# Forming only half of a real-input DFT's rows in the spectral layer, with the sums and differences on VectorE and GpSimd

## The chip, the cores and the metric

The kernel runs on one core of a Trainium2 chip. The metric is the time of one execution on the device in microseconds (us), as the median over several runs. The engines are named as the profile names them: PE is the TensorE matmul, DVE is VectorE, ACT is ScalarE, POOL is GpSimd. DMA is the memory transfer. SBUF holds the tiles that loads fill and operations read; PSUM holds what the matmuls write.

## The reference

The program runs four layers in the order A, B, A, B. Each adds its output to its input:

```python
x = x + A(layernorm(x), w_r, w_i)
x = x + B(layernorm(x), mem0, Wq, Wk, Wv, Wo)      # recurrent attention, not touched by the change
x = x + A(layernorm(x), w_r, w_i)
x = x + B(layernorm(x), mem0, Wq, Wk, Wv, Wo)

def A(x, w_r, w_i):                                 # x: 1 x 2048 x 640, bf16
    X = rfft2(x.astype(float32))                    # 2048 x 321 complex
    return irfft2(X * (w_r + 1j * w_i), s=(2048, 640)).astype(bfloat16)
```

## The kernel before

Layer A computes the transforms by matmuls with tables. The 2048 tokens are written as n = 16·s1 + s0. There are three stages, and the document uses these names throughout:

- **first transform**: normalise, then a transform over s1, with s1 on the partitions; the results lie in `YT`.
- **spectrum**: sixteen row groups `kg`; for each, the transform along d (640 to 321 frequencies), the transform across s0 (`K`), the complex filter, and the transform back across s0, to `UT`.
- **token stage**: for each of the sixteen s0, the transform back along d, the transform back over s1, the residual, the layernorm for layer B, and sums that layer B needs.

The first execution of layer A is called A1 here, the second A2. The parts that matter (cut; `...` marks the cuts):

```python
# first transform: 256 columns for each s0 (real and imaginary part of 128 rows)
nc.tensor.matmul(ps[...256 columns...], lhsT=xn[:, s0, ch * 128:(ch + 1) * 128], rhs=T[:, s0, :], start=True, stop=True)
...
# spectrum: 16 groups of 20 + 4 + 6 matmuls
for kg in range(16):
    ...
    for ch in range(5):
        for cin in range(2):
            lhsT = YT[:, ch, cin * 16 + kg, :, :].rearrange("p s k -> p (s k)")
            for cout in range(2):
                nc.tensor.matmul(ps[:, cout, 0:NF], lhsT=lhsT, rhs=Fd[:, ch, FD_IDX[(cin, cout)], :], start=(n == 0), stop=(n == 9))
            n += 1
    Z = ...; nc.scalar.copy(out=Z[:], in_=ps[:, :, 0:NF])
    ps3 = ...                                   # four matmuls with K: across s0
    nc.vector.tensor_tensor(out=t1[:], in0=ps3[:, :, 0:NF], in1=wr[:]..., op=ALU.mult)         # 642 elements
    nc.vector.tensor_tensor(out=t2[:], in0=ps3[:, ::-1, 0:NF], in1=wi[:]..., op=ALU.mult)      # 642 elements
    nc.vector.tensor_tensor(out=Xp[:, 0, 0:NF], in0=t1[:, 0, :], in1=t2[:, 0, :], op=ALU.subtract)
    nc.vector.tensor_tensor(out=Xp[:, 1, 0:NF], in0=t1[:, 1, :], in1=t2[:, 1, :], op=ALU.add)
    ...                                         # six matmuls back across s0
    nc.scalar.copy(out=UT[:, :, kg, :], in_=psuf[:, 0:768].rearrange("p (a k) -> p a k", k=8))
...
handoff.prefetch()                              # issues layer B's Wv, 5 x 1 MB, on GpSimd
# token stage: 12 + 8 matmuls for each s0; the residual is added on VectorE
for q in range(8):
    xr = wk.tile([128, 2, D], BF16, name="xr", tag="xr", bufs=4)
    nc.sync.dma_start(out=xr[:], in_=xs[:, 2 * q:2 * q + 2, :])
    xo = wk.tile([128, 2, D], BF16, name="xo", tag="xo")              # two buffers
    for t in range(2):
        ...
        nc.vector.tensor_tensor(out=xo[:, t, :]..., in0=psy[:, :, 0:320], in1=xr[:, t, :]..., op=ALU.add)
        _ln_stats(nc, st, mv, xo[:, t, :], t)
    nc.sync.dma_start(out=xd[:, 2 * q:2 * q + 2, :], in_=xo[:])       # the store of the layer's result
    ...
```

## Time and profile before

| | before |
|---|---|
| median of three runs (range) | 1765.64 us (1764.94 to 1770.21) |
| span of the profiled run | 1762.3 us |
| A1: first transform, spectrum, token stage | 40.4, 73.6, 58.7 us |
| A2: same (the first counted from the end of layer B) | 31.7, 73.5, 58.5 us |
| the rest, nearly all layer B | some 1400 us |

The head of the profile page gives the busy time of each engine and its share of the span:

```profile
span 1762.3 us, 36912 instructions
PE 1664.0 (94%) x14778; PEld 1136.0 (64%) x14779; DVE 863.2 (49%) x2432; ACT 816.8 (46%) x2234; POOL 222.9 (13%) x180
```

The share over the whole span says that PE is the limit, but what a change in layer A is worth is read from layer A's own stretches. In this view of stretches each line is one stretch: its bounds, its length, then the busy time of each engine (number of instructions), the granted PE clock, the share of time that the DMA engines were busy, and their GB/s.

```profile
core 0: us, PE busy (x) PEld busy (x) DVE busy (x) ACT busy (x) POOL busy (x), PEclk, DMA share, GB/s
0.00:40.40 40.40, 15.93 (x81) 9.75 (x83) 23.41 (x112) 21.41 (x30) 4.12 (x13) 0.82 0.68 157
40.40:114.00 73.60, 69.95 (x480) 44.62 (x479) 40.23 (x76) 22.67 (x32) 10.47 (x17) 0.98 0.61 152
114.00:172.70 58.70, 51.62 (x405) 33.46 (x405) 41.08 (x113) 25.90 (x48) 1.19 (x2) 0.97 0.56 206
914.00:987.50 73.50, 70.66 (x480) 44.85 (x480) 39.83 (x71) 21.98 (x32) 6.34 (x12) 0.96 0.44 94
```

In the spectrum (second line, and A2's in the fourth) PE is busy 70 of 73.6 us and DVE 40: PE is the limit, and removing matmuls there should pay. In the token stage PE is busy 51.6 of 58.7, and DVE 41. (A2's token stage, 58.5 us, reads the same.) The timeline shows the spectrum in detail; its columns are the start, the duration, the engine, the source line, the operation, output and inputs, and, in brackets, any idle time before it and what ended that.

```profile
74.94 0.30 PE L206 MATMUL ps<-Z,K 128*128 128x321 bf16 x1
75.22 2.36 PE L199 MATMUL ps<-Fd,YT 128*128 128x321 bf16 x16
...
79.25 0.30 PE L206 MATMUL ps<-Z,K 128*128 128x321 bf16 x1
```

One row group takes 79.25 − 74.94 = 4.31 us, and no line of it has a bracket: PE never waits. Sixteen of these make up the spectrum. On DVE, two lines of the same stretch:

```profile
75.43 0.83 DVE L210 TENSOR_TENSOR t<-ps,wr 128x642 f32<-128x642 f32 x1
76.17 0.82 DVE L211 TENSOR_TENSOR t<-ps,wi 128x642 f32<-128x642 f32 x1
```

Each lasts 0.82 to 0.83 us. Last, what the residual addition (L261) waited for, as time and number of times:

```profile
  DMA xr<-x: 9.2, 1
  DMA xr<-in_A_x_dram: 9.0, 1
```

In each layer A, DVE sits idle 9 us at the beginning of the token stage, until the first `xr` has landed. SyncE's queue (SPq) issued these loads 4.4 us after the first of the five `Wv` loads (108.8):

```profile
113.19 1.85 SPq L238 DMA_DIRECT2D xr<-in_A_x_dram  x4
```

PE itself lost only 1.99 us by it (1.55 in A2).

### The profile page before, as it was taken

The numbers are of one execution on the slowest core, as the hardware profiler recorded it, in microseconds if no ns is written. First come the engines' busy times: TensorE is split into PE (matmuls) and PEld (weight loads), VectorE is DVE, ScalarE is ACT, GpSimd is POOL, SyncE is SP. The second block draws the span as 40 slices with busy tenths as digits, with TensorE's granted clock in tenths as the row PEclk, the third lists the DMA queues.
The fourth block names the chain that finished last, engine by engine and source line by source line (L and its number), as shares of the span: only waits on it lengthen the run. The fifth ranks groups of instructions, "written<-read, shape, count | busy, mean of one in ns | idle before, by whom it ended". The sixth has DMA issues, their size and how long they took to land. (4 is left out here: it accounts for less than half of the span.)

```text
span 1762.3 us, 36912 instructions
## 1 busy us (share of the span) xinstructions
PE 1664.0 (94%) x14778; PEld 1136.0 (64%) x14779; DVE 863.2 (49%) x2432; ACT 816.8 (46%) x2234; POOL 222.9 (13%) x180
## 2 busy tenths in 40 slices
PE   4988899999999999999959889999999999999998
PEld 2655666666666666677736556666666666666776
DVE  5557255555455455443345572555555555555111
ACT  4334466656656656400023343656656656653000
POOL 0110011211211211200000000211211211211000
PEclk8999999999999999999979999999999999999999
DMA  6664034344344343374165540334434434424531
GB/s 144 158 239 157 14 105 148 115 148 148 116 147 148 117 149 123 113 236 146 53 158 99 202 142 17 129 121 137 151 124 137 152 122 136 145 108 140 186 128 32
DMA packets 148013, 233.11 MB, mean 132 GB/s; under 512 B 8480, under 2 KB 119664, under 8 KB 138096
## 3 DMA queue, kind: packets, MB, share of 16 engines
q1 hardware_dynamic: 141632, 203.72, 34.6%
q0 software_dynamic: 6192, 26.86, 6.0%
q8 instruction: 120, 1.97, 0.5%
q14 instruction: 69, 0.57, 0.1%
HBM read 191.30 MB, written 50.35 MB: 137 GB/s over the span
## 5 line engine op out<-in xcount | busy, mean ns | idle before, releaser
L755 DVE TENSOR_TENSOR P<-E,maskf 128x269 bf16<-128x269 bf16 (+5 forms) x576 | 199.6, 355 | 350.1 <-ACT E L754 350.1
L741 PE MATMUL psv<-wWv,hTf 128*128 128x256 bf16 x2720 | 340.4, 272 | 0.0
L678 PE MATMUL psk<-hTf,wWk 128*128 128x495 bf16 (+3 forms) x1600 | 324.3, 342 | 0.7 <-DVE hTf L970 0.7
L754 ACT ACTIVATE E<-pss 128x269 bf16<-128x269 f32 (+5 forms) x576 | 246.3, 429 | 152.0 <-PE pss L751 144.3
L678 PE MATMUL psq<-hTf,wWq 128*128 128x128 bf16 (+3 forms) x1560 | 314.3, 336 | 0.0
L743 ACT CAST V<-psv 128x512 bf16<-128x512 f32 (+1 forms) x288 | 162.0, 563 | 236.8 <-PE psv L741 236.8
L741 PEld LDWEIGHTS <-hTf 128*128 128x128 bf16 x2720 | 252.9, 98 | 24.6
L781 POOL TENSOR_TENSOR accS<-accS,sums_sb 128x634 f32<-128x634 f32 x64 | 98.3, 1536 | 931.3 <-ACT sums_sb L772 931.3
L734 DVE CAST KT<-psk 128x495 bf16<-128x495 f32 (+3 forms) x320 | 191.2, 598 | 41.9 <-PE psk L678 41.8
L502 PE MATMUL psx<-Wo_sb,oTxl 128*128 128x320 bf16 x1440 | 203.4, 299 | 0.0
L678 PEld LDWEIGHTS <-wWk 128*128 128x128 bf16 x1600 | 133.5, 97 | 96.6 <-issue 1.4
L751 PEld LDWEIGHTS <-KT 128*128 128x128 bf16 x1216 | 113.6, 98 | 116.4 <-issue 16.3
L678 PEld LDWEIGHTS <-wWq 128*128 128x128 bf16 x1580 | 127.0, 97 | 88.6 <-issue 1.1
L502 PEld LDWEIGHTS <-oTxl 128*128 128x128 bf16 x1440 | 140.9, 98 | 54.7
L719 ACT ACTIVATE QT<-psq 128x480 bf16<-128x480 f32 x300 | 170.0, 567 | 0.0
L751 PE MATMUL pss<-QT,KT 128*128 128x132 bf16 (+8 forms) x1216 | 159.5, 216 | 2.7 <-ACT E L754 2.6
L793 DVE TENSOR_TENSOR oT<-pso,oT 128x480 bf16<-128x480 f32 (+1 forms) x160 | 93.2, 583 | 60.3 <-PE pso L789 49.7
L789 PE MATMUL pso<-P,V 128*128 128x132 bf16 (+8 forms) x1216 | 120.1, 216 | 2.6 <-DVE oTmf L795 2.5
L516 DVE TENSOR_TENSOR xo<-psx,xr 128x320 bf16<-128x320 f32 x64 | 31.4, 490 | 177.1 <-PE psx L502 177.1
L793 DVE TENSOR_TENSOR oT<-pso,Rb 128x480 bf16<-128x480 f32 (+1 forms) x160 | 93.0, 581 | 48.9 <-PE pso L789 48.9
L199 PE MATMUL ps<-Fd,YT 128*128 128x321 bf16 x640 | 104.4, 306 | 4.4 <-DMA Fd<-cFd 2.8
L502 PE MATMUL psx<-Wo_sb,oT 128*128 128x320 bf16 x608 | 98.7, 302 | 4.1 <-DVE oT L793 4.1
(169 smaller groups left out, 1745.1 us busy)
## 6 DMA issues: line engine op xcount, KB each, us to landing
oT<-Rd SPq DMA_DIRECT2D x32, 1059.5 KB
Rb<-Rd SPq DMA_DIRECT2D x32, 1059.5 KB
oTx_d<-oT SPq DMA_DIRECT2D x60, 512.0 KB
oTxl<-oTx_d SPq DMA_DIRECT2D x18, 1024.0 KB
Wv_sb<-in_B_Wv_dram POOLq DMA_DIRECT2D x10, 1024.0 KB, 9.7
wWq<-in_B_Wq_dram SPq DMA_DIRECT2D x32, 320.0 KB
wWk<-in_B_Wk_dram SPq DMA_DIRECT2D x32, 320.0 KB
wWv<-in_B_Wv_dram SPq DMA_DIRECT2D x32, 320.0 KB
```

The costliest lines, as they stand in the source:

```text
L199: nc.tensor.matmul(ps[:, cout, 0:NF], lhsT=lhsT, rhs=Fd[:, ch, FD_IDX[(cin, cout)], :], start=(n == 0), stop=(n == 9))
L502: self.tc.nc.tensor.matmul(ps[:, 0:320], lhsT=lhs(h, k // 2 % 4), rhs=self.g["Wo_sb"][:, h, c0:c0 + 320], start=(h == 0), stop=(h == H - 1))
L678: nc.tensor.matmul(ps, lhsT=w[:, ch, hh * 128:(hh + 1) * 128], rhs=src[:, ch, lo:hi], start=(ch == 0), stop=(ch == 4))
L719: nc.scalar.mul(out=qv[:, :, 0:SEG], in_=x_view(ps, o, n)[:, :, 1:SW], mul=scale)
L734: nc.vector.tensor_copy(out=KTs[h % 2][:, lo:hi], in_=ps[:, 0:hi - lo])
L741: nc.tensor.matmul(ps[:, i * 256:(i + 1) * 256], lhsT=hT[:, ch, (t + i) * 128:(t + i + 1) * 128], rhs=w["Wv"][:, ch, :], start=(ch == 0), ...
L743: nc.scalar.copy(out=V[:, t:t + n, :].rearrange("p a b -> p (a b)"), in_=ps[:, 0:n * 256])
L751: nc.tensor.matmul(ps[:, off - o0:off - o0 + hi - lo], lhsT=KT[:, t * 128:(t + 1) * 128], rhs=QT[:, lo:hi], start=True, stop=True)
L754: nc.scalar.activation(out=E[:, 0:n], in_=ps[:, 0:n], func=ACTF.Exp)
L755: nc.vector.tensor_tensor(out=P[:, o0:o0 + n], in0=E[:, 0:n], in1=bs.mask[:, o0:o0 + n], op=ALU.mult)
L789: nc.tensor.matmul(pso[:, lo - q0:hi - q0], lhsT=V[:, t, (h % 2) * 128:(h % 2 + 1) * 128], rhs=P[:, off:off + hi - lo], start=(i == 0), st ...
L793: nc.vector.tensor_tensor(out=oT[:, s0 * SEG:(s0 + ns) * SEG].rearrange("p (s t) -> p s t", t=SEG), in0=po[:, :, 0:SEG], in1=pr[:, :, 0:SE ...
```

## The change

The input is real, so the transform over s1 and s0 has a symmetry: the rows for group 16 − j are conjugates of those for group j. The changed kernel forms only groups 0 to 8 of 16. The cosine and sine parts along d are computed once for each group, and their sums and differences give both the group and its mirror. The intent is to halve the matmuls along d and back along d. The price is elementwise work: a sum and a difference ahead of the transform across s0, and a sum and a difference after the filter. They go to VectorE and GpSimd. In the token stage the residual is added on PE, with an identity matrix, as the first two matmuls into the output's PSUM. In A1 the normalisation moves from VectorE to ScalarE, and the one-element copies that order a load after an earlier use of its buffer (the "gates", L108) do so everywhere. The core of the diff, with cuts:

```diff
 # first transform: 128 columns instead of 256
-        for j in range(4): nc.tensor.matmul(ps[... 256 columns], lhsT=xn[...], rhs=T[:, s0, :], ...)
+        for i in range(4): nc.tensor.matmul(ps[:, i, :], lhsT=xn[...], rhs=T[:, 4 * q + i, :], ...)
-                _ln_apply(nc, wk, mv, xt, xn[:, 4 * q:4 * q + 4, :], 4, eps_t, on_dve=True)
+                _ln_apply(nc, wk, mv, xt, xn[:, 4 * q:4 * q + 4, :], 4, eps_t)
...
 # spectrum: 8 steps j instead of 16 groups kg
+    def along_d(j, o):          # o=0 cosines, o=1 sines: 10 matmuls each; o=1 is copied to SBUF by ScalarE
+    def combine(j):
+        nc.vector.tensor_tensor(out=P[j][:, 0:2, :], in0=ac[:, :, 0:NF], in1=db, op=ALU.add)
+        nc.vector.tensor_tensor(out=P[j][:, 2:4, :], in0=ac[:, :, 0:NF], in1=db, op=ALU.subtract)
+    def across(j, sg):          # sg=0 the group, sg=1 its mirror: 4 matmuls each, into ONE buffer X
+    def filt(j, sg):            # two 642-element multiplications on VectorE for each sg
+    def products(j, sum_engine):
+        nc.vector.tensor_tensor(out=a[:, 0, :, :], in0=t1[j][:, :, 0, :], in1=t2[j][:, :, 0, :], op=ALU.subtract)
+        nc.gpsimd.tensor_tensor(out=a[:, 1, :, :], in0=t1[j][:, :, 1, :], in1=t2[j][:, :, 1, :], op=ALU.add)
+        if j:
+            sum_engine.tensor_tensor(out=sd[j][:, 0:2, :], in0=a[:, :, 0, :], in1=a[:, :, 1, :], op=ALU.add)
+            nc.gpsimd.tensor_tensor(out=sd[j][:, 2:4, :], in0=a[:, :, 0, :], in1=a[:, :, 1, :], op=ALU.subtract)
+    def back(j):                # for three chunks of frequencies: 4 matmuls into one of 2 buffers, 2 ScalarE copies
+        for j in range(8 + 3):
+            if j < 8:        along_d(j, 1)
+            if 1 <= j <= 8:  across(j - 1, 0); filt(j - 1, 0)
+            if j < 8:        along_d(j, 0); combine(j)
+            if 1 <= j <= 8:  across(j - 1, 1)
+            if j >= 3:       back(j - 3)        # and up to two late weight loads, issued on GpSimd
+            if 1 <= j <= 8:  filt(j - 1, 1); products(j - 1, nc.vector if j >= 7 else nc.gpsimd)
...
 # token stage: 6 + 6 matmuls for each s0
-    nc.vector.tensor_tensor(out=xo[:, t, :]..., in0=psy[:, :, 0:320], in1=xr[:, t, :]..., op=ALU.add)
+    for a in range(2):
+        nc.tensor.matmul(psy[:, a, 0:320], lhsT=g["ident"][:], rhs=xr[q][:, t, a * 320:(a + 1) * 320], start=True, stop=False)
+    ...                         # four matmuls with Ti
+    nc.scalar.copy(out=halves(xo[q][:, t, :]), in_=psy[:, :, 0:320])
```

The mirrored filter rows (`Wm`) are gathered by two indirect loads.

## The prediction

> **What bounds it now.** In the windows layer A takes 349 of 1762 us: A1 is 0-172.7 (first transform 40.4, spectrum 73.6, token stage 58.7), A2 884-1046 (15.0 waiting for xn, then 15.0, 73.5, 58.5). Layer B is untouched. In the spectrum PE is the limit: busy 69.95 of 73.6 us, DVE 40.2, ACT 22.7; the timeline repeats every 4.30 us, 16 times, with 30 matmuls, 0.137 us apart at 321 columns. In the token stage PE is busy 51.6 of 58.7, after a stall on the first residual load (DVE idle 9.0 us on DMA xr).
>
> **What changes.** Matmuls per layer: first transform 80 of 256 columns become 80 of 128; spectrum 16 x 30 become 8 x 40; tokens 16 x 20 become 16 x 12. PE work is then about 8 x (28 x 0.137 + 12 x 0.116) = 42 us in the spectrum and 16 x (1.64 + 0.34) = 32 us in the token stage.
>
> PE stops being the only limit of the spectrum. DVE gets seven 642-element operations per step j; two of that size take 826 and 815 ns now, so 5.8 us a step. (The Trainium skill, "VectorE: DVE Perf Modes", section on the SBUF-source errata: an fp32 add of two tensors takes (N+151)/0.96 ns, 826 for 642; the trace agrees.) GpSimd gets three adds; its 634-element add takes 1.536 us, so 4.65 us a step plus weight issues (0.5-0.9 each). The single X buffer makes a loop: filter half 0 (1.66), across half 1 (0.6), back with two PSUM buffers (1.9), along d (1.37), across half 0 (0.6), handovers: 6.3-6.5 us. Eight steps of 5.9-6.5 us, 4.5 to fill, about 10 to drain (last GpSimd difference, back(7), copy): 59 us against 73.6.
>
> Token stage: PE 2.15-2.3 us a row, ACT about 1.65 (two 0.69 copies), DVE 1.9, so PE still. The residual now goes first into PSUM, so PE itself waits for xr, issued only when the spectrum ends, beside 5 MB of Wv: 4-6 us lost, partly cold (the Trainium skill, "TensorE: Matmul & The Clock Gate", Part 1: half clock after an idle window of about 3.4 us[...]). Total 48 against 58.7.
>
> First stage: A1 moves the normalisation to ACT and splits the copies: about 33 against 40.4. A2 reads half the T table and its copies halve, but the mirrored filter is gathered ahead of Fd, and K is six times larger: the spectrum starts about 6 us earlier.
>
> **Sum.** A1 -33, A2 -31: 1765.6 - 64, about 1702 us (-3.6%). Nearly all is critical. Interval 1678 to 1728. Faster by over 2%: 0.93; within 2%: 0.06; slower: 0.01.
>
> **What would show it.** Spectrum windows of 55-63 us, DVE busy near 85%, PE 70-75% and waiting on DVE; GpSimd add near 1.55 us; token windows 45-50 us, PE about 75%, one wait on xr of 4-6 us; first spectrum matmul near 33 us in A1; later stages unchanged, shifted.
>
> **What would make it wrong.** GpSimd and DVE slowing each other (the products run together from SBUF), with GpSimd the limit at over 6.5 us a step; K or the gather landing late in A2; Wv or writes saturating DMA in the shorter token stage (13 MB in 48 us; 206 GB/s now); PE gaps dropping the clock to half through the spectrum. Upwards: steps of 5.8 us give another 5 us a layer.

## The result, and the profile after

The changed kernel took 1709.43 us (median of four runs, 1704.61 to 1711.07), the kernel before 1765.97 in the runs beside it. The ratio is 0.9671, with a 95% interval of 0.9645 to 0.9697: 3.3% faster. Ratios here and below are the mean time of one kernel's runs over the mean of the other's in the same rounds, so not quite the ratio of the medians quoted. The same file (e0 below) gave 1708.39.

The page and the stretches after, in the same views and columns:

```profile
span 1709.3 us, 35729 instructions
PE 1577.4 (92%) x14202; PEld 1085.8 (64%) x14203; DVE 838.0 (49%) x2315; ACT 809.5 (47%) x2327; POOL 288.9 (17%) x228
```

```profile
0.00:36.90 36.90, 11.47 (x81) 7.25 (x83) 23.64 (x86) 21.23 (x41) 6.61 (x19) 1.00 0.66 173
36.90:101.90 65.00, 48.85 (x320) 32.26 (x321) 43.83 (x58) 21.80 (x71) 38.28 (x31) 0.95 0.48 127
101.90:147.50 45.60, 32.97 (x277) 22.66 (x276) 27.93 (x97) 24.78 (x48) 3.74 (x7) 0.84 0.80 300
886.30:947.60 61.30, 48.66 (x320) 32.30 (x321) 46.41 (x57) 21.52 (x66) 34.53 (x26) 0.92 0.33 72
947.60:992.50 44.90, 32.47 (x277) 22.15 (x276) 27.54 (x97) 24.38 (x49) 3.86 (x7) 0.90 0.81 304
```

PE lost 86.6 us of busy time (1664.0 − 1577.4), and the span 53. The difference is in the stretches: in the spectrum PE is now busy 48.9 of 65 us and DVE 43.8 (67%; 76% in A2, where 85% was predicted), and no engine is full; in the token stage PE is busy 33 of 45.6. By stretch:

| us | A1 before | A1 after | predicted | A2 before | A2 after | predicted |
|---|---|---|---|---|---|---|
| first transform (A2: from layer B's end to the spectrum) | 40.4 | 36.9 | 33 | 31.7 | 26.1 | 25.7 |
| spectrum | 73.6 | 65.0 | 59 | 74.3 | 61.3 | 59 |
| token stage | 59.2 | 45.7 | 48 | 58.9 | 45.0 | 48 |
| transposes to layer B's first matmul | 13.6 | 13.2 | | 13.2 | 14.0 | |

(Here every bound is the start of the first matmul of its kind, so the A2 spectrum and the token stages are up to 0.8 us off the round bounds used above.) The differences add up to −26.1 and −31.7 us. Layer B's two passes add +4.0 and +0.8, though nothing in them was changed; together −53.0, the difference of the two profiled spans. Layer B's first pass varied from 693.9 to 703.4 us between the profiled runs that have the same instructions there. So stretches of layer A are compared below rather than totals alone, where a few us matter. Why layer B varies stays open.

The stretches vary too. In the profiles that have the same instructions there, the spectrum took 64.4 to 65.1 us in A1 and 61.2 to 62.0 in A2, A1's first transform 36.7 to 37.4, the transposes 13.2 to 14.1. Each edit below has one profile, so a difference under 1 us is not read as an effect.

**A step of the spectrum.** The step repeats every 6.13 us:

```profile
68.32 0.72 PE L326 MATMUL X<-YT,K 128*128 128x321 bf16 x4 [0.34 <-DVE t L334]
68.89 1.03 PE L360 MATMUL psu<-K,YT 128*128 128x256 bf16 x8
70.22 0.60 PE L360 MATMUL psu<-K,YT 128*65 128x256 bf16 x4 [0.30 <-ACT UT L362]
70.65 1.54 PE L301 MATMUL ab<-Fd,YT 128*128 128x321 bf16 x10
72.03 0.71 PE L326 MATMUL X<-YT,K 128*128 128x321 bf16 x4
72.58 1.53 PE L301 MATMUL ab<-Fd,YT 128*128 128x321 bf16 x10
74.45 0.72 PE L326 MATMUL X<-YT,K 128*128 128x321 bf16 x4 [0.34 <-DVE t L334]
```

PE waits twice in a step: 0.34 us at the second `across`, because `X` has one buffer and the filter (L334) must empty it, and 0.30 us at the last chunk of `back`, because that stage has two PSUM buffers and ScalarE must empty one. In the rest of the step, 5.48 us, PE is busy. DVE is not full either:

```profile
68.18 0.82 DVE L314 TENSOR_TENSOR YT<-ab,GT 128x642 bf16<-128x642 f32 x1
68.92 0.82 DVE L315 TENSOR_TENSOR YT<-ab,GT 128x642 bf16<-128x642 f32 x1
69.65 1.55 DVE L334 TENSOR_TENSOR t<-X,Wm 128x642 f32<-128x642 f32 x2
...
72.83 1.56 DVE L334 TENSOR_TENSOR t<-X,WX 128x642 f32<-128x642 f32 x2 [0.70 <-PE X L326]
```

Its operations last 0.82 us and start 0.735 us apart, so seven of them take 7 × 0.735 = 5.15 us, and DVE itself waits 0.70 us for the next `X`. The single `X` is a loop of PE and DVE waiting for each other in turn.

**The end of the spectrum.** From the first to the last matmul group that writes `X(j, 0)` (the first `across` of a step) the seven intervals take 40.5 us in A1 (43.03 to 83.50) and 41.1 in A2. After the start of the last one come 18.4 us in A1 and 14.5 in A2 before the token stage can begin; this holds the whole eighth step. In A1 most of this is one wait of PE:

```profile
92.14 1.26 PE L326 MATMUL X<-YT,K 128*128 128x321 bf16 x4 [7.92 <-DVE t L334]
```

PE waits for DVE's filter; DVE in turn waited for GpSimd, since the sum of step 6 (L345), which the kernel puts on DVE near the end, stands ahead of the next filter in DVE's queue and needs GpSimd's addition (L343):

```profile
89.78 0.83 DVE L345 TENSOR_TENSOR YT<-ac 128x642 bf16<-128x642 f32 x1 [5.14 <-POOL ac L343]
90.53 1.55 DVE L334 TENSOR_TENSOR t<-X,WX 128x642 f32<-128x642 f32 x2
```

And GpSimd had what that addition needs (the filter, done by about 83.5) nearly 5 us before it got there, because its queue is in order and was behind:

```profile
78.00 0.90 POOL L1181 DMA_DIRECT2D Wo_sb<-in_B_Wo_dram  x1 [2.71 <-ACT Wo_sb L108]
...
82.39 1.56 POOL L343 TENSOR_TENSOR GT<-t,t 128x642 f32<-128x642 f32 x1
84.47 0.58 POOL L1035 DMA_DIRECT2D maskf<-mask_f_B_f  x1 [0.52 <-ACT m L108]
...
87.62 0.57 POOL L1037 DMA_DIRECT2D m<-in_B_mem_dram  x1
88.20 1.55 POOL L343 TENSOR_TENSOR ac<-t,t 128x642 f32<-128x642 f32 x1
```

The line at 78.00 shows the start of it: the issue of a weight load waited 2.71 us for its gate, a ScalarE copy of one element (L108). So the arithmetic behind the load waited too. In A2 there are no `Wo` loads, and PE's wait is 4.00 instead of 7.92.

**GpSimd and VectorE slow each other.** Where a GpSimd operation and a VectorE operation with both inputs in SBUF start together, the one that starts second takes much longer. From A2, DVE then POOL:

```profile
926.51 2.21 DVE L342 TENSOR_TENSOR GT<-t,t 128x642 f32<-128x642 f32 x1
```

```profile
926.49 1.55 POOL L343 TENSOR_TENSOR GT<-t,t 128x642 f32<-128x642 f32 x1 [0.96 <-DVE t L334]
```

The subtraction that takes 0.83 us alone took 2.21. In the reverse order, at 95 us in A1, DVE's took 0.83 and GpSimd's addition 2.19 instead of 1.55. In both cases the pair needed 2.23 us from the first start to the last end, nearly the sum of both durations (0.83 + 1.55 = 2.38). DVE's filters, one of whose inputs is in PSUM, stayed at 0.81 to 0.83 us beside GpSimd work. The Trainium skill ("SBUF — State Buffer", section "SBUF: two separate sides") says that VectorE and GpSimd share a pair of SBUF ports, that a VectorE operation with two SBUF inputs needs it against a GpSimd operation that reads SBUF, and that it "is an exclusive lock, not a bandwidth split", the one that starts first holding it for its whole instruction. The trace agrees.

**The token stage.** The predicted wait of PE for `xr` was only 0.66 us. The first `xr` loads are now issued 0.5 us ahead of `Wv` (101.76) and not 4.4 us behind it:

```profile
101.27 5.58 SPq L256 DMA_DIRECT2D xr<-in_A_x_dram  x5
```

A larger wait came instead, and in ACT's timeline it stands like this:

```profile
120.48 0.69 ACT L241 CAST xo<-psy 128x640 bf16<-128x640 f32 x1 [8.58 <-DMA x<-xo]
```

ACT writes the fifth row of output, the first into a buffer `xo` that is used a second time, and waits 8.58 us until the store of its former content (`x<-xo`) has landed; PE, out of PSUM buffers behind it, idles 6.97 us (6.40 in A2). The groups view of L241 sums the waits up for the whole kernel:

```profile
  DMA x<-xo: 18.0, 3
```

The store was issued at 107.8; 5 MB of `Wv` had been issued from 101.8. From 104 to 120 us the DMA engines are fully busy, with 407 to 424 GB/s; in this stretch of 4 us PE does nothing at all:

```profile
116.00:120.00 4.00, 0.00 (x0) 0.00 (x0) 0.00 (x0) 0.00 (x0) 0.00 (x0) 0.52 1.07 418
```

In the kernel before, `Wv` was issued at 108.8 and the first store 16.1 us later, at 124.9, when most of `Wv` had landed; there it was the `xr` loads that stood behind `Wv`. After the change the store comes only 6.0 us after `Wv`. The Trainium skill ("DMA: Bandwidth & Descriptors", section "Issuing engines are not separate DMA queues") says that transfers issued by different engines run on the same 16 DMA engines and interleave; that agrees with a store issued by SyncE being slowed by loads that GpSimd issued. After the stall PE runs at half clock (0.26 to 0.27 us for a matmul, against 0.137), as the prediction expected after such a gap (6.97 us here). So long a gap is not always needed: in the kernel before, the matmuls at 116.6 also took 0.47 us instead of 0.30, after gaps of only 2.19 and 0.89 us.

### The profile page after: what moved, and what is told of

Same layout as the page of the kernel before. It is cut to its first block, busy times and chain, and to the rows that moved or that the text cites. A ratio compares the mean times of both kernels' runs of the same rounds, so it can differ in the third digit from the quotient of the medians. Undisturbed runs are those within 1.5% of the kernel's fastest.

```text
span 1709.3 us, 35729 instructions
## 1 busy us (share of the span) xinstructions
PE 1577.4 (92%) x14202; PEld 1085.8 (64%) x14203; DVE 838.0 (49%) x2315; ACT 809.5 (47%) x2327; POOL 288.9 (17%) x228
## 5 line engine op out<-in xcount | busy, mean ns | idle before, releaser
L902 PEld LDWEIGHTS <-V 128*128 128x128 bf16 x1216 | 92.4, 99 | 15.3 <-DVE oTmf L908 8.2
## 6 DMA issues: line engine op xcount, KB each, us to landing
Wv_sb<-in_B_Wv_dram POOLq DMA_DIRECT2D x10, 1024.0 KB, 13.2
```

The source lines that it names most:

```text
L902: nc.tensor.matmul(pso[:, lo - q0:hi - q0], lhsT=V[:, t, (h % 2) * 128:(h % 2 + 1) * 128], rhs=P[:, off:off + hi - lo], start=(i == 0), st ...
```

## The experiments

Twelve runs followed: eleven edits of the changed kernel, and the changed kernel once more (e0). Every one gave the right result. Diffs are against the changed kernel. "Stretches" are those of the table above. In short:

| kernel | median us (range) | ratio to before | 95% |
|---|---|---|---|
| changed | 1709.43 (1704.61–1711.07) | 0.9671 | 0.9645–0.9697 |
| e0, changed again | 1708.39 (1706.21–1710.08) | 0.9669 | 0.9655–0.9683 |
| e1, four `xo` | 1692.84 (1692.11–1694.89) | 0.9585 | 0.9572–0.9599 |
| e2, sums on GpSimd to the end | 1706.20 (1704.28–1708.83) | 0.9664 | 0.9649–0.9679 |
| e3, `Wo` issued by SyncE | 1711.09 (1707.47–1715.61) | 0.9691 | 0.9672–0.9710 |
| e4, residual on DVE | 1724.00 (1722.95–1726.36) | 0.9762 | 0.9748–0.9776 |
| e5, normalisation on DVE | 1704.52 (1703.16–1707.24) | 0.9653 | 0.9639–0.9668 |
| e6, `Wv` later | 1708.90 (1707.04–1713.03) | 0.9679 | 0.9663–0.9696 |
| e7, `back` split | 1711.17 (1707.27–1714.31) | 0.9688 | 0.9673–0.9704 |
| e8, nothing on GpSimd | 1721.37 (1719.51–1723.44) | 0.9749 | 0.9735–0.9763 |
| e9, e1+e2+e3+e7 | 1691.08 (1686.04–1693.67) | 0.9577 | 0.9563–0.9590 |
| e10, e1+e3+e7 | 1692.72 (1690.98–1696.41) | 0.9583 | 0.9569–0.9596 |
| e11, three `xo`, six `xr`, e2+e3+e5+e7 | 1706.93 (1702.38–1709.90) | 0.9658 | 0.9638–0.9678 |

### e1: four buffers for the output row pair

Theory: the token stage stalls on the second use of an `xo` buffer. Rival: DMA is simply full there, and another buffer only moves the wait.

```diff
-                xo[q] = wk.tile([128, 2, D], BF16, name="xo", tag="xo")
+                xo[q] = wk.tile([128, 2, D], BF16, name="xo", tag="xo", bufs=4)
```

> The token tile xo gets four buffers instead of two. Theory (ACT may not overwrite an xo buffer until its store has landed, and the store waits in the DMA queues behind 5 MB of Wv): the ACT wait on DMA x<-xo (8.6 us in A1 of the changed kernel, 18 us in all) nearly goes, the token windows of 45.6 and 44.9 us shrink to 38-40, the kernel is 10 to 14 us faster than the changed one (about 1697). Rival (DMA saturation itself paces the stage, whoever waits): the wait moves to the residual loads xr or to later stores, the token windows stay over 43 us and the time within 4 us of the changed kernel.

Measured: 1692.84 us, about 16.6 less than the changed kernel. The token stages fell from 45.7 and 45.0 to 38.3 and 38.1 us; the first transforms and the spectra stayed within 0.3 us. What L241 waited for, after the edit:

```profile
  DMA x<-xo: 1.7, 2
```

18.0 us became 1.7. What remains on PE is a wait of 2.08 and 1.98 us for `xr`. The two stretches explain 7.4 + 6.9 = 14.3 us of the total; the rest is inside layer B's variation. The theory holds as far as PE goes: with more buffers PE no longer waits for the store. That the store is slow because of the traffic is another matter, for e6.

### e2: the last sums on GpSimd as well

Theory: DVE's queue is blocked by the sum that waits for GpSimd.

```diff
-                products(j - 1, nc.vector if j >= 7 else nc.gpsimd)
+                products(j - 1, nc.gpsimd)
```

> The sums of the last two steps go back from VectorE to GpSimd. Theory (VectorE runs in order, and its sum of step 6 stands in front of the filter of step 7 and waits for GpSimd's add, which is late): DVE no longer idles 5.1 us on POOL, PE's wait of 7.9 us before the second half of step 7 falls under 3 us in A1, although GpSimd gets two adds of 1.3 us more; the spectrum windows (65.0 and 61.3 us) shorten by 1 to 4 us each. Rival (the move to VectorE did shorten the drain, as it was meant to): both windows grow by 1 to 3 us, because the last GpSimd difference comes later by one or two adds.

Measured: 1706.20 us. PE's wait fell from 7.92 to 1.95 us in A1 (4.00 to 3.07 in A2), but GpSimd then ends later, and PE waits 1.80 us for it. The spectrum is shorter by 1.2 and 2.0 us only. So the wait at L345 was really what made the 7.92, but removing it uncovers GpSimd's own backlog as the next limit. The total alone, 2 to 3 us lower with overlapping intervals, does not show it.

### e3: the Wo loads issued by SyncE

Theory: the weight loads in GpSimd's queue, with their gates, hold up the arithmetic.

```diff
-        nc.gpsimd.dma_start(out=g["Wo_sb"][:, 8 * q:8 * q + 8, :], ...)
+        nc.sync.dma_start(out=g["Wo_sb"][:, 8 * q:8 * q + 8, :], ...)
```

> The four Wo loads are issued from SyncE instead of GpSimd (they need no cast); only A1 has them. Theory (GpSimd's adds are late in A1 because its queue also issues these loads, each after a wait for a gate copied on ACT): the A1 spectrum window falls from 65.0 to about 61 us, that of A2 (61.3), with PE's longest wait near A2's 4.0 us; A2 unchanged; the kernel 3 to 5 us faster. Rival (the lock between VectorE and GpSimd[...] alone makes the stall): A1 stays at 64-66 us.

Measured: 1711.09 us in total, not resolved from the changed kernel. PE's wait in A1 fell from 7.92 to 4.97, the spectrum of A1 by 1.6 us (65.0 to 63.4); A2, which has no such loads, stayed at 61.2. I had expected about 4 us. The trace says why: the `Wo` issues are gone, but the next load, of the mask, now holds the queue:

```profile
85.74 0.57 POOL L1035 DMA_DIRECT2D maskf<-mask_f_B_f  x1 [2.31 <-ACT m L108]
```

So the theory is half right: issues in that queue do cost, but removing one kind of them uncovers the next.

### e4: the residual back on VectorE

This undoes one part of the change. Theory: PE has time for two more matmuls a row, DVE does not have it for a 0.82 us addition.

```diff
-            for a in range(2):
-                nc.tensor.matmul(psy[:, a, 0:320], lhsT=g["ident"][:], rhs=xr[q][...], start=True, stop=False)
-            nc.scalar.copy(out=halves(xo[q][:, t, :]), in_=psy[:, :, 0:320])
+            nc.vector.tensor_tensor(out=halves(xo[q][:, t, :]), in0=psy[:, :, 0:320], in1=halves(xr[q][:, t, :]), op=ALU.add)
```

> The residual is undone: no identity matmuls, VectorE adds xr while it evacuates psy (0.82 us), ACT only copies psg. VectorE then has about 2.75 us a row (0.82 + 1.1 statistics + 0.75 norm) against PE 1.7: if VectorE limits, the token stage after its store stall runs at 2.7 us a row instead of 1.80, the token windows grow to 55-58 us, and the kernel is 18 to 24 us slower than the changed one, 1728-1734. Rival (PE-bound, the residual on PE costs time): the windows shorten by 16 x 0.27 = 4 us each.

Measured: 1724.00 us, 14.6 more. The token stages took 52.3 and 53.4 us. In a stretch of the same steady part, DVE is the full engine and PE is not:

```profile
128.00:140.00 12.00, 8.47 (x78) 5.46 (x75) 11.41 (x32) 3.55 (x8) 0.00 (x0) 1.00 0.42 155
```

In the changed kernel PE is busy 12.00 of the same 12 us, DVE 10.93, and a row takes 1.80 us; here it takes 2.6. The stretches are shorter than expected (55 to 58) because the slower rows hide part of the store's wait: PE stalls 4.75 and 4.13 us here, instead of 6.97 and 6.40. With all else as in the changed kernel, the residual on PE is thus worth about 15 us.

### e5: the normalisation of A1 back on VectorE

Theory: A1's first transform is 4 us longer than predicted because ScalarE normalises more slowly (0.905 us for a row of 640, against DVE's 0.44; the expectation below has the distances between starts). Rival: it does not matter where it runs.

```diff
-                _ln_apply(nc, wk, mv, xt, xn[:, 4 * q:4 * q + 4, :], 4, eps_t)
+                _ln_apply(nc, wk, mv, xt, xn[:, 4 * q:4 * q + 4, :], 4, eps_t, on_dve=True)
```

> In A1 alone VectorE normalises the rows again, as before, instead of ACT (0.84 us a row on ACT here, 0.38 on VectorE). Theory (the first stage of A1 is a chain statistics - ACT - small VectorE operations - normalisation - transform for each quarter, and the normalisation of four rows stands in it with 3.4 us instead of 1.5): the first spectrum matmul comes at 33.5-35.5 us instead of 36.9. Rival (the stage is limited by the in-order queues of ACT and VectorE, and VectorE gets 6 us more): it comes at 37-39 us. Nothing else moves; the kernel within 4 us of 1709.

Measured: the first transform took 35.9 us instead of 36.9, between the two expectations. Neither holds: 1 us of the 4 is where the normalisation runs. (e11, with the same edit, has 36.0; the eleven profiles without it have 36.7 to 37.4.) The trace says why it is so little: DVE's queue now holds the normalisation too, and the last quarter's statistics end at 30.2 us instead of 22.7. The total of 1704.52 is lower by more than that, but its profile also has the shortest pass of layer B (693.9), so it is not counted.

### e6: Wv issued later

Theory: the store's wait comes from the `Wv` traffic; if `Wv` comes later, the wait is gone.

```diff
-        if handoff is not None:
-            handoff.prefetch()
 ...
                 nc.sync.dma_start(out=xd[:, 2 * q:2 * q + 2, :], in_=xo[q][:])
+            if s0 == 5:
+                handoff.prefetch(xo[q][0:1, t, 0:1])      # each load behind a gate on this row
```

> The five Wv loads wait for row 5 of the token stage instead of starting with it; xo keeps two buffers. Theory (the stores, and with them ACT, wait only because Wv's 5 MB are ahead of them in the DMA engines): the wait of ACT on DMA x<-xo of 8.6 us goes as with four xo buffers, token windows 38-41 us, Wv still lands before its use some 15 us after the stage, time 1692-1700. Rival (a store's own latency with two buffers is the limit): a wait of over 4 us stays at the third store and the windows stay over 43 us.

Measured: 1708.90 us, the same as the changed kernel; as expected, the wait at 121 us is gone, but against the expectation it came back later. ACT and POOL, from the timeline:

```profile
130.23 0.69 ACT L239 CAST xo<-psy 128x640 bf16<-128x640 f32 x1 [7.03 <-DMA x<-xo]
```

```profile
115.59 2.68 POOL L1190 DMA_DIRECT2D Wv_sb<-in_B_Wv_dram  x5 [16.94 <-ACT Wv_sb L108]
```

Stores issued before `Wv` (from 108.0 on) were not waited for; those behind it were, by 7.03 and once more by 3.84 us. So the expected gain did not come: the token stages took 47.2 and 46.0 us, in the range of the rival, though not with its wait at the third store. Yet the run shows that the long wait follows `Wv` wherever it is put. It also tests another rival, the `xr` loads ahead of the store in SyncE's own queue: here the first store, issued at 107.98, stood behind the same five `xr` loads but ahead of `Wv`, and ACT wrote its buffer at 112.30 without a wait for it, 4.3 us later, where the changed kernel needed 12.7. Together with e1: `Wv` makes the store slow, two buffers make PE feel it.

### e7: the chunks of `back` apart

Theory: the step is set by the two handovers seen above (0.34 and 0.30 us) and not by an engine's work. Put between them, work that is there anyway hides them.

```diff
+            if j >= 3:
+                back(j - 3, (0,))          # first chunk of frequencies
             if 1 <= j <= 8:
                 across(j - 1, 1)
             if j >= 3:
-                back(j - 3)
+                back(j - 3, (1, 2))
```

> The first of the three chunks of back moves ahead of the second across: it fills PE's wait on VectorE (0.34 us a step) and gives ACT time to free the PSUM buffer (0.30 us a step). Theory (the steady step of 6.12 us is the loop through the single X buffer, VectorE idle 0.7 us in it): the step falls to 5.6-5.9 us in the middle of the spectrum. Whether the window shortens depends on GpSimd, which has about 5.4 us of work a step and the stall at the end: 0 to 2 us each. Rival (VectorE or GpSimd throughput limits the step): the step stays at 6.1 us. Time within 4 us of 1709.

Measured: the step fell from 6.13 to 5.38 us, below the expected range, with no wait on PE:

```profile
61.73 0.72 PE L326 MATMUL X<-YT,K 128*128 128x321 bf16 x4
...
67.11 0.72 PE L326 MATMUL X<-YT,K 128*128 128x321 bf16 x4
```

In the stretch between these two lines PE is busy all the time:

```profile
61.73:67.11 5.38, 5.38 (x41) 3.79 (x41) 5.28 (x9) 2.77 (x10) 5.29 (x6) 1.00 1.07 217
```

So without the two handovers PE is the limit of the step again, and DVE and GpSimd, busy for 5.28 and 5.29 us of it, are close behind. But the spectrum of A1 became no shorter (66.1 against 65.0); A2's did (59.2 against 61.3). In A1 PE then waits, from 78 us on, 2.43 and 3.59 us on DVE and 0.85 to 0.99 us six more times, four of these for GpSimd: at the end GpSimd's queue, which also issues the loads, is the last. The total, 1711.17 (six runs), is not resolved from the changed kernel. A faster step was given back at the end of the spectrum.

### e8: all of it on VectorE

Theory: GpSimd is worth having despite the lock. Rival: since the two engines exclude each other for these operations, VectorE alone does as well.

```diff
-        nc.gpsimd.tensor_tensor(out=a[:, 1, :, :], ...)          # and the sum and the difference
+        nc.vector.tensor_tensor(out=a[:, 1, :, :], ...)
```

> All products, sums and differences go to VectorE; GpSimd only issues loads. VectorE then has ten operations a step, started 0.735 us apart in the trace: step 7.4-7.7 us instead of 6.12, 77 operations in all or 56.6 us; no waits on GpSimd, no subtraction of 2.2 us, a drain shorter by some 4 us. Theory (the offload to GpSimd pays in the steps and is given back in part at the end): windows of 66-70 us against 65.0 and 61.3, the kernel 4 to 12 us slower. Rival (GpSimd costs more than it brings): windows of 58-63 us, the kernel faster.

Measured: 1721.37 us, 12 more than the changed kernel, as the theory expected. The spectrum takes 69.1 and 68.8 us, in steps of 7.61 us with a wait for DVE in each:

```profile
67.06 0.72 PE L326 MATMUL X<-YT,K 128*128 128x321 bf16 x4 [1.82 <-DVE t L334]
...
74.67 0.59 PE L326 MATMUL X<-YT,K 128*128 128x321 bf16 x3 [1.83 <-DVE t L334]
```

Ten operations in 7.61 us are 0.76 us each: DVE is full. The gain of the offload is less than the difference of the steps, 7 × (7.61 − 6.13) = 10.4 us a layer, since the stretches differ by 4.1 and 7.5 us only: without GpSimd there is less waiting at the end.

### e9, e10, e11: the parts together, and the changed kernel once more

e9 joins e1, e2, e3 and e7. e10 is e9 without e2. e11 has three `xo` buffers and six `xr`, and e5 as well (four `xo` with eight `xr` did not fit into SBUF, so it was not run). e0 is the changed kernel unedited, to have it in the same batch.

```diff
 # e9
+ tag="xo", bufs=4   ;   products(j - 1, nc.gpsimd)   ;   Wo by nc.sync   ;   back(j - 3, (0,)) ahead of across(j - 1, 1)
 # e10: the same without products(j - 1, nc.gpsimd)
 # e11: the edits of e9 but tag="xo", bufs=3 ; tag="xr", bufs=6 ; and on_dve=True in A1's normalisation
```

> The changed kernel once more, unedited, to stand beside the next three on the same chip: 1704-1711 us; windows of layer A within 0.5 us of its first profile (36.9, 65.0, 45.7; 26.1, 61.3, 45.0), and what differs from it lies in layer B, whose first pass took 695 to 703 us in the profiles so far with the same instructions.

> Four xo buffers, sums on GpSimd, Wo issued from SyncE, back split. If the store stall, the stall on GpSimd and the X loop are separate causes, the gains add where GpSimd allows: token windows 38 us; spectrum 60-62 us in A1 and 57-59 in A2 (65.0 and 61.3); 1684-1691 us in all. Rival: GpSimd limits the spectrum now (5.2-5.6 us of work and lock a step), the windows stay at 63 and 59 as with the sums alone, 1688-1693.

> As e9_best, but the last two sums stay on VectorE. If VectorE's wait in order for GpSimd's add is what makes that placement bad, also with the faster steps: spectrum windows 2 to 4 us longer than in e9_best each, 4-8 us in all. Rival: with back split GpSimd is so late that taking two adds off it is worth more: windows 1-2 us shorter than in e9_best.

> As e9_best, with A1's rows normalised on VectorE and three xo and six xr buffers (four and eight do not fit) against the residual wait of 2 us that four xo buffers left. If that wait is only a matter of loads issued too late: token windows 36-37 us, A1's spectrum starting 1 us earlier, 3 to 5 us less than e9_best. Rival: the DMA engines are full while Wv comes, and more loads ahead of the stores bring back a wait on x<-xo: token windows 38-41 us.

Measured: e0's stretches were 37.3, 64.4 and 45.8 us in A1 and 26.1, 62.0 and 45.7 in A2, up to 0.7 off the first profile, more than the 0.5 expected. e9 took 1691.08 us, the fastest: 4.2% faster than before, 1.0% faster than the changed kernel of the same batch (1708.39). Its stretches:

```profile
36.90:97.10 60.20, 48.27 (x320) 31.83 (x321) 44.63 (x56) 21.78 (x71) 35.77 (x29) 0.97 0.51 137
97.10:135.20 38.10, 32.05 (x277) 22.24 (x276) 27.57 (x97) 24.64 (x48) 3.76 (x7) 0.90 0.95 358
```

The spectrum took 60.3 and 59.1 us, the token stage 38.1 twice, and there DMA is now busy 95% of the time. Against e1 the total is not resolved (the intervals overlap), though the spectra are shorter by 4.4 and 2.3 us; the spans differ, but layer B varies by more. e10's spectra are 1.7 and 0.8 us longer than e9's; I had expected 2 to 4 each. The direction is that of e2, but e11, which has e9's spectrum, differs from e9 by as much as 1.4 us, so the size is not resolved, nor is the total, 1.6 us. e11 has good spectra (58.9 and 59.7), but its token stages took 46.6 us: the store's wait of PE was back, with 5.94 and 5.66 us. So with three `xo` buffers, and more `xr` loads ahead in the queue, nothing is left of e1's gain. The run changed both at once, so it does not say which of them did it.

## Why the prediction was right or wrong

The interval held, and 1709.43 is 7.4 us above the predicted 1702. What bound the kernel was read rightly: PE work was removed in layer A, where PE was the limit, and the gain came there (57.8 us in its stretches, for 86.6 us less of PE work). The terms of the sum, one by one:

1. **"A2 ... the spectrum starts about 6 us earlier": right**, 5.6 us. Counted from the end of layer B, 2.0 us come from the first matmul, which waits less for `xn` (14.7 instead of 16.7 us), 1.9 from the issue of `Fd`, now 1.8 instead of 3.7 us after that matmul, and 1.7 from the time between the issue and the spectrum (9.6 instead of 11.3 us; `Fd` has two tables instead of three). PE's last wait is for `Fd`, as before (3.87 us, before 2.82). One of the two gathers is ahead of `Fd`, as stated; what it costs was not tested.
2. **"First stage: A1 ... about 33": mis-sized, 36.9.** One of the 4 us is the normalisation on ScalarE (e5). The other three are not settled. In the trace ScalarE's queue, which is in order, holds copies and normalisation ahead of the last quarter's layernorm, whose statistics end at 22.7 us and whose first ScalarE operation starts at 27.93. That this is the cause is argued, not tested.
3. **"Eight steps of 5.9-6.5 us": nearly right, 6.13.** The loop around the single `X` was the right mechanism, as the two waits on PE and e7 show. "5.8 us a step" for DVE was too much: the durations were read from the trace, but the distance between starts is what counts for a full engine, and it is 0.735 us, so 5.15. The page that the prediction named ("VectorE: DVE Perf Modes") gives the duration, 826 ns, with which the trace agrees; the overlap was visible in the profile before, at L210 and L211, and I did not read it. But the 59 us are not the sum of the text's own terms: eight steps of 5.9 to 6.5 with 4.5 and 10 at the ends give 62 to 66.5, and the measured 65.0 and 61.3 lie in that range or just under it. The 59 come out with seven steps only (44.5 us for these). Measured, the seven intervals took 40.5 and 41.1 us, because the first two, before `back` begins, took only 5.3; the fill took 6.2 and 5.8, with PE at half clock (0.27 us for a matmul) in a part of it.
4. **"About 10 to drain": here the mechanism was missing.** After the start of the last `X(j, 0)` came 18.4 and 14.5 us. The eighth step is in that; without it (6.1 us) the drain took 12.3 us in A1 and 8.4 in A2. Its size was thus missed by some 2 us each way, and so near only by luck, since it was sized by the work left. What it really holds is the backlog of GpSimd's in-order queue: load issues with gates among the arithmetic, then a sum on VectorE that waits for GpSimd with the filter waiting behind it (e2, e3), and the two engines excluding each other. The text had named "GpSimd and DVE slowing each other" as a risk for every step. It occurred, with 2.2 us for a pair, but in the steady steps it did not set the pace.
5. **"PE itself waits for xr ... 4-6 us lost": wrong in its object, and by accident near in its size.** `xr` cost 0.66 us. The text put it beside 5 MB of `Wv`, as before the change, but its first loads are now issued 0.5 us ahead of `Wv`. Another wait, for the store of `xo` behind `Wv`, cost 6.97 and 6.40 us of PE (e1, e6). The text had "Wv or writes saturating DMA in the shorter token stage" among what could go wrong; it went wrong in that way, not through the mean rate that it calculated (13 MB in 48 us), but through a collision: the first rows no longer wait for `xr` and come faster, so the first store is issued 6.0 us after `Wv` (107.8 and 101.8) instead of 16.1.
6. **"PE 2.15-2.3 us a row": too much, 1.80.** PE is busy without a gap in the steady rows, so no handover has to be added. That saved some 6 to 8 us and paid for the stall: 45.7 and 45.0 us against the predicted 48.

In sum the predicted −33 and −31 became −26.1 and −31.7, and layer B's variation adds the rest. Two errors in the token stage cancelled in part, so the total was better than its parts.

## What to carry to other kernels

When a stage gets faster, look at what then meets in time: a small store behind a large prefetch costs little while its buffer isn't needed, and 7 us of matmul time in each layer once it is; more buffers (e1) were worth 17 us, beside the 56 of the whole change. Size an engine's load from the distance between starts and not from durations, and size the end of a pipeline from its queues in order, not from the work left. Offloading to GpSimd paid (12 us), but load issues in its queue wait for their gates and hold the arithmetic behind them.

## What the Trainium skill lacked or had wrong

- "SBUF — State Buffer", section "SBUF: two separate sides": right about the exclusive lock; a size for this pair is not there. A 642-element fp32 subtraction on VectorE went from 0.83 to 2.21 us behind a GpSimd addition of 1.55, and the addition from 1.55 to 2.19 in the other order; the pair takes 2.23 us.
- "GPSIMD Engine Reference", section "Elementwise — side-by-side cycle accounting": its two-input figures are for fp32. With the same 642 fp32 inputs, an fp32 output took 1.55 us and a bf16 output 1.32.
- "DMA: Bandwidth & Descriptors", sections "Issuing engines are not separate DMA queues" and "SWDGE vs HWDGE vs iDMA": that transfers interleave is right, and the second adds that each DMA engine goes round between the queues fed by GpSimd and by SyncE. Read so, one would not expect a long wait for a small store. Here a store of 0.33 MB, issued 6 us after 5 MB by GpSimd and behind five equal-sized loads of `xr` in its own queue, was waited for until 12.7 us after its issue. In e6, with the same five loads ahead of it but without the prefetch, it took no more than 4.3 us, so most of the 12.7 is the prefetch. Why the sharing is so uneven stays open.
- The same page gives about 1 us for the first byte of a load issued by GpSimd. No run here shows a first byte; what the trace shows is how long the issue keeps GpSimd busy, 0.90 us for each `Wo` load and 0.57 for the mask. No page gives what such issues cost the arithmetic behind them in GpSimd's queue: here an issue waited for its gate for up to 2.71 and 2.31 us, and the arithmetic with it.
